# Another written order of the same 1,474 jobs in a fused cosformer-attention and SwiGLU kernel on one core

## The chip, the cores and the metric

One core of a Trainium2 chip runs the whole kernel; the other seven are not used. The metric is the device time of one execution in microseconds. Lower is better. The core's engines are named as in the profile: PE is the matrix engine and PEld its weight load, DVE the vector engine, ACT the scalar engine, POOL the GpSimd engine and SP the sync engine, which here only issues transfers.

## The reference

Linear attention over 8 batches, 8 heads, 576 positions and 64 features per head, and a gated feed-forward block on its result:

```python
def _attn_ref(q, k, v):
    theta = np.pi / 2.0 * np.arange(S) / S              # S = 576
    phi = lambda x: concat([relu(x) * cos(theta), relu(x) * sin(theta)], axis=-1)
    q_p, k_p = phi(q), phi(k)
    kv = einsum('bhsf,bhsd->bhfd', k_p, v)
    den = einsum('bhsf,bhf->bhs', q_p, k_p.sum(axis=2)) + 1e-06
    return einsum('bhsf,bhfd->bhsd', q_p, kv) / den[..., None]

def _moe_ref(x, w_gate, w_val, w_out):                  # x: 4608 x 512
    g = x @ w_gate                                      # 512 x 1536
    return (g * sigmoid(g) * (x @ w_val)) @ w_out       # 1536 x 512
```

The attention output, 4,608 tokens of 512, is the input of the feed-forward block; the result is 4,608 x 512 in float32.

## The kernel before

The 4,608 tokens form nine groups of 512, and a group four tiles of 128. A tile of attention output is a pair of matmul batches into two PSUM banks (`tile_jobs`, lines 768 to 823): PE multiplies the turned query features by the key-value sums, ACT scales the denominators (L803), DVE inverts them (L809) and multiplies (L820), and the tile is turned, by PE for the first tiles (L757) and by a transposing transfer for the others (L749). The key-value sums of a batch are one PE job of 72 small matmuls (`kv_job`, L718) with four casts behind it (L630 on ACT, L634 on DVE). The query features of a batch need its query load (`raw_q`, L125 and L128) and two activations per position slot (L880, L890).

The feed-forward block of the first group is plain: for each of 12 blocks of 128 columns of `w_gate` and `w_val` a PE job of four matmuls each (L917), a SiLU (L925) and a product into `ht` (L937); then 16 jobs of the output product with `w_out` (L1275), cut into four pieces of it by the time at which each piece of `wo_sb` lands. From the second group on the gate and value products (L990) and the output product (L1155) go by a seven-product block scheme, whose sums are made on DVE (L501, L963, L1106, L1010 to L1026) and whose copies are made on ACT (L630).

Up to line 548 the program is written out by hand in one list of words: it loads the first batch, makes the first four attention tiles and blocks 0 to 5 of the first group. All loads of weights and of batches 0 to 2 are issued on POOL ahead of what follows; they share eight completion semaphores, so a load is issued when the eighth before it has landed.

All that comes after is made as jobs, in the order in which the code creates them (number 0 to 1473), and each job has a list of jobs that it must follow. No scheduler runs: a table, `ORDER`, names every job once and so sets what each engine's queue holds and in which order. A word is the job's number, a letter where the job could run on ACT (`a`) or DVE (`v`), and behind the colon the PSUM banks or other places that it takes:

```python
for word in ORDER.split():
    n, e, at = re.match(r"(\d+)([av]?):?([\d,]*)", word).groups()
    j, at = jobs[int(n)], [int(x) for x in (at.split(",") if "," in at else at)]
    j.eng = {"a": "ACT", "v": "DVE", "": next(iter(j.engs))}[e]
    assert j.eng in j.engs and not todo.intersection(j.after + j.behind)
    for r in j.get:
        r.at, at = at[:r.n], at[r.n:]
    todo.remove(j)
    j.fn(j)
```

Each engine works through its own queue in that order. An instruction waits for the semaphores of the instructions that it depends on: its inputs, and those that used its PSUM bank or buffer last. The jobs that the prediction speaks of:

- 4, 8, 12, 16, 20, 24 are the gate products of blocks 6 to 11 of the first group, and 6, 10, 14, 18, 22, 26 the value products (L917). Job 20 is the first that reads the last piece of `wg_sb` (blocks 10 and 11).
- 34 is the key-value sum of batch 1, 35 to 38 its four casts.
- 72, 78, 89, 95 and 104 are the matmuls of attention tiles 4 to 8 (L784), and 67, 84 and 101 turn the queries for them (L1323).
- 39 to 54 are the plain output products (L1275); job 45 is the first that reads the third piece of `wo_sb` (blocks 4 to 7), job 48 the first that reads the last.
- 722 is the key-value sum of batch 6, 723 to 726 its casts, 701 the load of batch 7's query, and 891 an activation that makes features from it (L880).

Of the kernel before, what the change touches and what calls it, by code (L numbers as in the profile page):

```python
# [18 lines left out]
def kernel(  # L19
# [1403 lines left out]
    for tg in range(1, NTG):  # L1423
# [43 lines left out]
        8:7 4:2 12:4 6:1 16:3 10:0 20:5 24:6 5:0 9:5 21:7 13:1 25:3 17:2 29 26:5 22:2 14:7 186 28 7 191 11 31 30 1:0  # L1467
        32 33 67:6 2:4 34:01 68a 70a 38a 35a 36a 37a 223 27 15 219 3 69 71 23 0 39:3 18:5 40:4 78:671 72:120 19 220
        84:5 101:0 79 80 81:0 43 82:6 85a 73 83 87v 187 74 86 75:0 88 188 51:7 42 89:561 45 52 95:120 90 102a 96 91
# [106 lines left out]
```

## Time and profile before

| | before |
|---|---|
| median of 3 runs | 297.64 us |
| the 3 runs | 298.81, 297.64, 297.64 us |
| the profiled execution's own time | 296.95 us |
| its span in the trace | 294.9 us |
| busy PE, DVE, ACT, POOL | 289.7, 253.7, 203.9, 67.9 us |
| granted TensorE clock | 1.00 |
| moved by DMA | 40.91 MB, mean 139 GB/s |

The span runs from the first to the last instruction of the core; the 2.05 us between it and the execution's own time lie around the instructions. PE is counted as busy from a matmul's start to its modelled end, and the matmuls overlap, so a short wait between two of them does not show as idle time in the page; it shows in the timeline as a later start than the rows ahead would give.

### The profile page before, as it was taken

What the parts mean: (1) busy time and instruction counts of PE and PEld (TensorE: products, weight loads), DVE (VectorE), ACT (ScalarE), POOL (GpSimd) and SP (SyncE); (2) the same over time, 40 slices, a digit from 0 to 9 for tenths busy, and PEclk for the clock granted to TensorE, in tenths of its full rate; (3) what the DMA queues carried; (4) which work ended last, traced back from release to release, by engine and by line L of the source; (5) the groups of instructions that cost most, each with busy time, mean ns of one, the idle gap of its engine ahead of it and who ended that gap; (6) DMA issues with size and microseconds to landing.
All of it is one profiled execution on the core that took longest, in us unless ns stands there. A gap on an engine that the chain in (4) does not pass through costs nothing.

```text
span 294.9 us, 8252 instructions
## 1 busy us (share of the span) xinstructions
PE 289.7 (98%) x3328; PEld 241.6 (82%) x3328; DVE 253.7 (86%) x518; ACT 203.9 (69%) x430; POOL 67.9 (23%) x122
## 2 busy tenths in 40 slices
PE   8999999999999999999999999999999999999994
PEld 4597465768888888998898898888988988888883
DVE  8877689999997999999989987998879859966983
ACT  6562556989768987897789589976566275666530
POOL 6763530004008022052215120500050041000200
PEclk9999999999999999999999999999999999999999
DMA  7999999997995997989899994756260343000217
GB/s 252 235 195 198 202 206 208 181 234 113 186 203 134 171 212 111 175 174 172 128 194 198 159 153 81 154 111 83 33 161 19 39 96 86 2 0 2 71 27 190
DMA packets 71974, 40.91 MB, mean 139 GB/s; under 512 B 48768, under 2 KB 68736, under 8 KB 71936
## 3 DMA queue, kind: packets, MB, share of 16 engines
q0 software_dynamic: 24800, 24.39, 48.8%
q1 hardware_dynamic: 46528, 15.47, 28.8%
q10 hardware_dynamic: 608, 0.52, 0.7%
q8 instruction: 26, 0.43, 0.6%
q14 instruction: 12, 0.10, 0.1%
HBM read 37.75 MB, written 9.44 MB: 160 GB/s over the span
## 4 chain that ended last, share of the span: by engine, by line
PE 84%; DMA 14%; issue 0%; DVE 0%; POOL 0%; POOLq 0%
PE banks L990 49%; PE banks L1155 25%; DMA wg_sb<-in_moe_w_gate_dram 7%; DMA wo_sb<-in_moe_w_out_dram 4%; PE banks L1275 3%; PE banks L789 2%; PE banks L718 2%; DMA raw_q<-in_q_dram 2%; DMA wo_sb<-in_v_dram 1%; PE banks L1065 1%; PE banks L757 0%; PE banks L784 0%; DVE r_q L636 0%; POOL hold L469 0%; POOL raw_q L128 0%
## 5 line engine op out<-in xcount | busy, mean ns | idle before, releaser
L1124 POOL DMA_DIRECT2D out_dram<-ob x52 | 27.7, 540 | 125.0 <-ACT ob L632 49.6
L1085 DVE TENSOR_TENSOR ht<-sg,banks 128x512 f16<-128x512 bf16 x69 | 46.4, 681 | 3.3 <-PE banks L990 2.8
L1049 ACT ACTIVATE sg<-banks 128x512 bf16<-128x512 f32 x72 | 42.0, 595 | 6.0 <-PE banks L990 4.7
L630 ACT COPY banks<-banks 128x512 f32<-128x512 f32 (+1 forms) x56 | 31.8, 573 | 16.6 <-PE banks L990 6.1
L990 PEld LDWEIGHTS <-wg_sb 128*128 128x128 f16 x384 | 37.0, 98 | 5.3
L1155 PEld LDWEIGHTS <-ht 128*128 128x128 f16 x384 | 37.2, 98 | 4.6
L990 PEld LDWEIGHTS <-wgs_sb 128*128 128x128 f16 x380 | 36.8, 98 | 4.9 <-issue 0.2
L990 PEld LDWEIGHTS <-wv_sb 128*128 128x128 f16 x368 | 35.6, 98 | 4.3
L1010 DVE TENSOR_TENSOR banks<-m,banks 128x512 f32<-128x512 f32 x47 | 32.4, 691 | 5.5 <-PE banks L990 3.4
L990 PE MATMUL banks<-kvt,wgs_sb 128*128 128x256 f16 x248 | 35.4, 273 | 0.0
L630 ACT COPY m<-banks 128x512 f32<-128x512 f32 x47 | 26.9, 586 | 8.8 <-PE banks L990 7.8
L1155 PEld LDWEIGHTS <-sums 128*128 128x128 f16 x288 | 27.9, 98 | 3.4
L990 PE MATMUL banks<-xT,wg_sb 128*128 128x256 f16 x192 | 28.3, 272 | 0.0
L990 PE MATMUL banks<-xT,wv_sb 128*128 128x256 f16 x184 | 27.6, 273 | 0.0
L1155 PE MATMUL banks<-wo_sb,ht 128*128 128x256 f16 x192 | 24.9, 273 | 0.0
L1155 PE MATMUL banks<-wt_sb,sums 128*128 128x256 f16 x192 | 24.2, 273 | 0.0
L990 PE MATMUL banks<-kvt,wg_sb 128*128 128x256 f16 x168 | 23.9, 273 | 0.0
L632 ACT ACTIVATE ob<-banks 128x512 f32<-128x512 f32 x32 | 19.0, 597 | 7.1 <-PE banks L1155 5.7
L1155 PE MATMUL banks<-wt_sb,ht 128*128 128x256 f16 x192 | 23.2, 273 | 0.0
L820 DVE TENSOR_TENSOR x<-banks,rec 128x512 f16<-128x512 f32 x31 | 21.3, 689 | 1.9
L990 PE MATMUL banks<-kvt,wv_sb 128*128 128x256 f16 x160 | 22.2, 273 | 0.0
L890 ACT ACTIVATE r_q<-raw_q,tanq 128x256 bf16<-128x256 bf16 x45 | 20.5, 500 | 0.8 <-DMA phit<-r_q 0.6
(160 smaller groups left out, 526.1 us busy)
## 6 DMA issues: line engine op xcount, KB each, us to landing
out_dram<-ob POOLq DMA_DIRECT2D x52, 128.0 KB, 3.6
raw_kv<-in_k_dram POOLq DMA_DIRECT2D x7, 576.0 KB, 6.5
raw_q<-in_q_dram POOLq DMA_DIRECT2D x12, 288.0 KB, 10.6
raw_kv<-in_v_dram POOLq DMA_DIRECT2D x6, 576.0 KB, 9.8
out_dram<-ob SPq DMA_DIRECT2D x12, 128.0 KB, 3.0
wg_sb<-in_moe_w_gate_dram POOLq DMA_DIRECT2D x5, 256.0 KB, 9.0
wv_sb<-in_moe_w_val_dram POOLq DMA_DIRECT2D x5, 256.0 KB, 9.4
wo_sb<-in_v_dram SPq DMA_DIRECT2D x2, 576.0 KB, 4.1
```

The lines of the kernel that those rows point to most:

```text
L630: nc.scalar.copy(out=out, in_=in_)
L632: nc.scalar.mul(out=out, in_=in_, mul=mul)
L718: nc.tensor.matmul(out=ps[i * D:(i + 1) * D, e, jj * 2 * D1:(jj + 1) * 2 * D1], lhsT=raws[b, "k"][es, 2 * jj + i, c], rhs=v2s[b == 1][es, ...
L820: tt(out=x_.rearrange("p (i y d) -> p i y d" if pairs else "p (y e d) -> p e y d", d=D, **({"i": 2} if pairs else {"e": 2})), in0=view()[: ...
L890: nc.scalar.activation(out=home()[:, :, c, 1], in_=raws[b, "q"][:, :, c], func=AF.Relu, scale=tanq[:, c:c + 1])
L990: nc.tensor.matmul(out=to[:, i], lhsT=a[:, c, 2 * u + i], rhs=x()[:, :, c], start=first and i == 0 and c == 0, stop=c == KH - 1, skip_grou ...
L1010: tt(out=bank(c), in0=one(m7_all, m).rearrange("p i x -> p (i x)"), in1=bank(b), op=ALU.add)
L1049: nc.scalar.activation(out=gates(rooms[w])[:, :, jh * HT:(jh + 1) * HT], in_=src, func=AF.Silu, scale=DOWN)
L1085: tt(out=ht[:, 4 * u + w:4 * u + w + 3:2, jh * HT:(jh + 1) * HT], in0=gates(rooms[w])[:, :, jh * HT:(jh + 1) * HT], in1=src.rearrange("p ( ...
L1124: {"POOL": nc.gpsimd, "SP": nc.sync, "ACT": nc.scalar}[j.eng].dma_start(out=out_v[idx // NC, idx % NC][:, cols], in_=ob_of(t)[e * SH:(e + ...
L1155: nc.tensor.matmul(out=to, lhsT=a[:, kc, i * P:(i + 1) * P], rhs=b[:, kc], start=first and kc == 0 and i == 0, stop=kc == HC - 1, skip_gro ...
L1275: nc.tensor.matmul(out=bank(tiles[t]), lhsT=ht[:, fc, t * P:(t + 1) * P], rhs=wo_sb[:, fc], start=(fc == 0), stop=(fc == FC - 1))
```

## The change

The table `ORDER` is written anew, nothing else. The same 1,474 jobs stand in it, POOL's and SP's jobs in the same sequence as before, and the jobs of PE, DVE and ACT moved against each other by some places: no PE job moves by more than some 7 us of PE work. Most jobs that take a PSUM bank get another one, and two of the jobs that can run on either engine change it: a cast of batch 1's key-value sums (37) and a ReLU (85) go from ACT to DVE, and another ReLU (87) from DVE to ACT. The first line of the table before and after:

```diff
-        8:7 4:2 12:4 6:1 16:3 10:0 20:5 24:6 5:0 9:5 21:7 13:1 25:3 17:2 29 26:5 22:2 14:7 186 28 7 191 11 31 30 1:0
+        10:0 4:3 8:1 12:2 20:4 24:7 16:5 9:6 5:2 21:0 13:1 25:3 29 17:8 187 28 11 223 219 220 188 31 30 33 1:4 189 32
```

Three places show what that does to an engine's queue. In the rows a name in square brackets is a semaphore that the row waits for: DMASW those of loads issued by POOL, DMAHW those of SP's transfers, the others those of an engine.

PE, where the table's part of the program begins, before. DMASW0 is the landing of the last piece of `wg_sb`, DMASW1 that of the last piece of `wv_sb`:

```order
L917 LDWEIGHTS wg_sb [waits DMASW2_49]
L917 MATMUL banks<-xT,wg_sb 128x512 [waits DVE_49]
...
L917 LDWEIGHTS wg_sb [waits DMASW5_49]
...
L917 LDWEIGHTS wv_sb [waits DMASW3_49]
L917 MATMUL banks<-xT,wv_sb 128x512 [waits DVE_49]
...
L917 LDWEIGHTS wg_sb [waits DMASW0_49]
...
L917 LDWEIGHTS wv_sb [waits DMASW1_49]
```

and with the change:

```order
L917 LDWEIGHTS wv_sb [waits DMASW3_49]
L917 MATMUL banks<-xT,wv_sb 128x512 [waits DVE_49]
...
L917 LDWEIGHTS wg_sb [waits DMASW2_49]
L917 MATMUL banks<-xT,wg_sb 128x512 [waits DVE_49]
...
L917 LDWEIGHTS wg_sb [waits DMASW5_49]
...
L917 LDWEIGHTS wg_sb [waits DMASW0_49]
...
L917 LDWEIGHTS wv_sb [waits DMASW6_49]
```

The row that waits for DMASW0 is job 20. Ahead of it stood 24 matmuls of this list (jobs 8, 4, 12, 6, 16, 10); now 16 stand there (jobs 10, 4, 8, 12). It comes two jobs of four matmuls earlier.

PE, around the first product with the third piece of `wo_sb` (its landing is DMASW0 again), before: the tile of L784 is tile 6, and job 45 follows it.

```order
L784 LDWEIGHTS phit [waits Activation_49]
L784 MATMUL banks<-phit 128x65 [waits DVE_49]
...
L784 LDWEIGHTS phit [waits DVE_49]
...
L1275 LDWEIGHTS ht [waits DMAHW1_49]
L1275 MATMUL banks<-wo_sb,ht 128x512 [waits DMASW0_49]
```

and with the change, from tile 6 on:

```order
L784 LDWEIGHTS phit [waits DVE_49]
L784 MATMUL banks<-phit 128x65 [waits Activation_49]
...
L1323 LDWEIGHTS raw_q
L1323 MATMUL banks<-ident,raw_q 64x128
...
L784 MATMUL banks<-phit 128x65 [waits DVE_49]
...
L1275 LDWEIGHTS ht [waits DMAHW1_49]
L1275 MATMUL banks<-wo_sb,ht 128x512 [waits DMASW0_49]
```

Job 101 (8 small matmuls that turn tile 8's queries) and job 95 (tile 7) now stand between tile 6 and job 45.

ACT, at the first activation on batch 7's query, before. DMASW3 and DMASW2 are the two halves of that load, DMAHW2 the transfer that turns batch 6's features and so frees `r_q`; `kv` are the casts of batch 6:

```order
L630 CAST kv_0_191<-banks 64x4x65 [waits PE_49]
L630 CAST kv_0_191<-banks 64x4x65
L630 COPY banks<-banks 128x512 [waits DVE_49,PE_49]
L1049 ACTIVATE sg<-banks 128x2x256 [waits DVE_49]
L630 CAST kv_0_191<-banks 64x4x65
L880 ACTIVATE r_q<-raw_q,tanq 128x4x64 [waits DMAHW2_49,DMASW3_49,DMASW2_49]
```

and with the change:

```order
L630 CAST kv_0_191<-banks 64x4x65 [waits DVE_49,PE_49]
L630 CAST kv_0_191<-banks 64x4x65
L880 ACTIVATE r_q<-raw_q,tanq 128x4x64 [waits DMAHW2_49,DMASW3_49,DMASW2_49]
L1049 ACTIVATE sg<-banks 128x2x256 [waits PE_49]
L630 COPY banks<-banks 128x512 [waits DVE_49,PE_49]
```

The activation that waits for the load has moved ahead of a copy, a SiLU and a cast, and the key-value job (722) ahead of it stands four products of four matmuls earlier in PE's queue.

More of the change, by code (lines that the diff above doesn't have):

```diff
@@ L1466 @@
     ORDER = """
-        8:7 4:2 12:4 6:1 16:3 10:0 20:5 24:6 5:0 9:5 21:7 13:1 25:3 17:2 29 26:5 22:2 14:7 186 28 7 191 11 31 30 1:0
-        32 33 67:6 2:4 34:01 68a 70a 38a 35a 36a 37a 223 27 15 219 3 69 71 23 0 39:3 18:5 40:4 78:671 72:120 19 220
-        84:5 101:0 79 80 81:0 43 82:6 85a 73 83 87v 187 74 86 75:0 88 188 51:7 42 89:561 45 52 95:120 90 102a 96 91
[64 rows of a table removed]
+        10:0 4:3 8:1 12:2 20:4 24:7 16:5 9:6 5:2 21:0 13:1 25:3 29 17:8 187 28 11 223 219 220 188 31 30 33 1:4 189 32
+        6:2 14:6 22:0 26:1 67:3 34:45 70a 68a 15 7 23 27 69 37v 71 39:6 18:3 2:7 38a 35a 36a 3 0 19 72:450 78:011 79
+        73 80 81:1 84:2 42 40:7 43 82:0 51:3 52 87a 83 85v 74 86 88 75:0 89:011 90 190 186 224 91 92:3 101:2 95:450 45
+        102a 96 41:2 93:0 76:1 48 97 98:1 103 221 94 77 55:0 99:4 104:010 227:5 46 44 57 100 105 122 123 120 228:6 117
[64 rows of a table added]
     """
```

128 rows, old and new, of the table ORDER are left out of this document.

## The prediction

> **What bounds the kernel now.** I read the page's busy times and its chain first, then the windows, then the chain of waits in order of time, and last the timelines of PE, ACT and DVE where the chain leaves PE.
>
> From the page, busy time by engine, and the chain that ended last by engine:
>
> ```profile
> PE 289.7 (98%) x3328; PEld 241.6 (82%) x3328; DVE 253.7 (86%) x518; ACT 203.9 (69%) x430; POOL 67.9 (23%) x122
> PE 84%; DMA 14%; issue 0%; DVE 0%; POOL 0%; POOLq 0%
> ```
>
> PE carries 84% of the chain, transfers 14%, nothing else anything. Three stages of the windows (PE, PEld, DVE, ACT, POOL busy, clock, DMA share, GB/s):
>
> ```profile
> 30.00:40.00 10.00, 10.00 (x128) 5.18 (x126) 7.69 (x16) 5.58 (x11) 6.10 (x9) 1.00 1.31 202
> 100.00:110.00 10.00, 10.00 (x94) 8.96 (x92) 9.93 (x21) 9.05 (x19) 1.49 (x3) 1.00 1.19 193
> 250.00:260.00 10.00, 10.00 (x94) 8.96 (x93) 9.27 (x18) 6.88 (x14) 0.00 (x0) 1.00 0.01 2
> ```
>
> A stage of the block scheme starts 94 matmuls in 10 us at clock 1.00, at 100 us as at 250 us. PE is full, and DVE is nearly full beside it (9.93 of 10). The transfers of the chain, in order of time:
>
> ```profile
> 20.06 11.22 DMA wg_sb<-in_moe_w_gate_dram
> 31.80 12.82 DMA wo_sb<-in_moe_w_out_dram
> 44.66 1.46 PE banks L1275 x6
> ```
>
> The last piece of `wg_sb` lands at 20.06 + 11.22 = 31.28 us, the third piece of `wo_sb` at 31.80 + 12.82 = 44.62 us, and PE's product with it starts 0.04 us later. After that the chain stays on PE to the end. Now PE's timeline across the jobs that the table starts with:
>
> ```profile
> 27.27 2.75 PE L917 MATMUL banks<-xT,wg_sb 128*128 128x512 f16 x12
> 29.86 1.03 PE L917 MATMUL banks<-xT,wv_sb 128*128 128x512 f16 x4
> 32.45 1.89 PE L917 MATMUL banks<-xT,wg_sb 128*128 128x512 f16 x8
> 36.86 0.64 PE L1323 MATMUL banks<-ident,raw_q 128*64 128x128 bf16 x16
> 37.54 1.24 PE L718 MATMUL banks<-phit,raw_kv 64*64 64x130 bf16 x72
> 38.72 0.61 PE L1275 MATMUL banks<-wo_sb,ht 128*128 128x512 f16 x2
> 39.16 1.03 PE L917 MATMUL banks<-xT,wv_sb 128*128 128x512 f16 x4
> 40.02 0.59 PE L1275 MATMUL banks<-wo_sb,ht 128*128 128x512 f16 x2
> 40.55 0.42 PE L784 MATMUL banks<-phit 64*128 64x65 bf16 x16
> 40.90 0.22 PE L784 MATMUL banks<-kvt,phit 64*64 64x65 bf16 x2
> 41.28 0.86 PE L1323 MATMUL banks<-ident,raw_q 128*64 128x128 bf16 x24
> 42.08 0.61 PE L1275 MATMUL banks<-wo_sb,ht 128*128 128x512 f16 x2
> 42.52 0.39 PE L757 MATMUL banks<-ident,x 128*128 128x128 f16 x4
> 42.74 1.03 PE L1275 MATMUL banks<-wo_sb,ht 128*128 128x512 f16 x4
> 43.70 0.20 PE L784 MATMUL banks<-phit 64*128 64x65 bf16 x2
> 44.18 0.39 PE L784 MATMUL banks<-phit 64*128 64x65 bf16 x14 [0.28 <-DVE phit L1339]
> 47.29 1.03 PE L1275 MATMUL banks<-wo_sb,ht 128*128 128x512 f16 x4
> ```
>
> Starts matter here, not busy times. Twelve matmuls from 27.27 to 29.86 give 0.216 us each, or 0.864 us a job. Tile 5 takes 40.90 - 40.55 = 0.35 us; tile 6, begun at 43.70, is followed only at 44.66: 0.61 us lost, part of it to DVE's product at 44.18, the rest to the landing. That is the one wait of size after 27 us. Later ones are small; a typical one of the larger:
>
> ```profile
> 93.23 0.60 PE L990 MATMUL banks<-kvt,wg_sb 128*128 128x256 f16 x4
> 93.80 0.60 PE L990 MATMUL banks<-kvt,wv_sb 128*128 128x256 f16 x4
> ```
>
> Four matmuls at 0.109 us end 0.44 us after their start, and the next start is 0.57 us after: 0.13 us lost. I found some six waits of 0.03 to 0.15 us, 0.5 us in all. So what an order can win is bounded: 0.61 + 0.5, some 1.1 us, unless it shortens what lies ahead of 27.27 us or the jobs themselves, and it touches neither.
>
> The Trainium skill, "Perfetto Trace Analysis", section "Identifying the Most-Contended Engine", calls matmul busy time a bad measure and asks for the busy share of weight loads; by that rule PEld's 82% would leave PE 18% of the span to win. The trace does not bear it out: the starts show PE issuing at one pace almost throughout, at whatever share its weight loads stand.
>
> **The change part by part.** Durations are those of the profiled execution, whose own time is 296.95 us for a span of 294.9; the median of the three runs is 297.64, 0.69 above it, and I carry that difference unchanged.
>
> *First products.* Job 20 comes after 16 matmuls instead of 24: 27.27 + 16 x 0.216 = 30.73 us, where its piece of `wg_sb` lands at 31.28. With the 0.04 us seen at the other landing PE waits **0.59 us**. Before it came at 32.45, 1.17 us after the landing. Job 24 and everything else on PE queues up behind that wait, the value products 6 and 14 that could have filled it among them.
>
> *Third piece of `wo_sb`.* To tile 4 PE has eleven products (11 x 0.864 = 9.50), the first turn with the small product of the tangents (from 36.86 to 37.54, 0.68), the key-value sum (1.18), two output matmuls (0.44) and job 18 (0.86): 12.66 us, so it comes there at 27.27 + 12.66 + 0.59 = 40.52. From there to job 45 stand tile 4 (0.38), three tiles of 0.35, the turns of 24 small matmuls (0.80), one turned tile (0.22) and ten output matmuls (0.24 each as from 42.74 to 43.70, 2.40): 4.85 us, 45.37 us, or 0.75 us after the landing at 44.62. The **0.61 us go**. What would be late next is the last piece, job 48: it stands at 47.29 us before, with no gap ahead of it, and behind job 45 come its 0.86, two output matmuls (0.48) and two turned tiles (0.44): 47.15, within 0.15 us of the old moment. I take nothing.
>
> *First tiles.* A cast of batch 1's sums moves from ACT to DVE, and tile 4 waits for it. DVE's rows there:
>
> ```profile
> 35.50 1.41 DVE L292 TENSOR_TENSOR phit<-raw_kv,tab 128x1152 bf16<-128x1152 bf16 x2
> 37.17 1.27 DVE L937 TENSOR_TENSOR ht<-sg,banks 128x512 f16<-128x512 bf16 x2
> 38.78 0.74 DVE L1339 TENSOR_TENSOR phit<-phit,tanT 128x512 bf16<-128x512 bf16 x2
> ```
>
> From the same 35.50 DVE now does two L292 with a copy of 0.21 and a weight sum of 0.41 among them (1.41 + 0.62 less 0.16 of overlap: 37.37), four L937 (two take 1.27, so 0.60 each: 39.75), one L1339 (0.37) and the cast (ACT does one in 0.38): 40.4 us, against PE's 40.52. It fits by 0.1 us, and only because PE was held 0.59 us; were that wait shorter, this one would take up to 0.4 us of it. Cost zero, bounds 0 and 0.4.
>
> *Batch 7's query.* ACT's first use of it moves ahead. The rows: PE's key-value sum of batch 6, ACT's casts behind it and first use, the two loads, and how long they took:
>
> ```profile
> 167.92 1.25 PE L718 MATMUL banks<-v,raw_kv 64*64 64x130 bf16 x72
> 169.21 0.76 ACT L630 CAST kv<-banks 64x260 bf16<-64x260 f32 x2 [2.38 <-PE banks L718]
> 171.88 0.51 ACT L880 ACTIVATE r_q<-raw_q,tanq 128x256 bf16<-128x256 bf16 x1
> L125 POOL DMA_DIRECT2D raw_q<-in_q_dram x2: 652/664/677, 158.3 to 159.0; - x2
> DMA to landing us min/median/max: 9.5/9.9/10.3
> ```
>
> The query is there by 159.0 + 10.3 = 169.3 us; before, its user came 2.6 us later. Now the key-value sum is four products of 0.44 earlier (166.2), its casts end at 166.2 + 1.29 + 0.76 = 168.2, and ACT then stands 1.1 us waiting for the landing. Queued behind it are a SiLU (0.60) and the copy (0.57) on which an output product on PE waits: ready at 169.3 + 0.41 + 0.50 + 0.57 = 170.8. PE has the 72 small matmuls (1.18) and 40 large ones (4.36) ahead of that product and comes at 166.2 + 5.54 = 171.7. It hides behind 0.9 us of PE work: zero here, and one for one beyond that.
>
> *All the rest*, some 450 PE jobs in a new mixture. A job's inputs come through ACT and DVE in the same counts and at the same durations, so I take the 0.5 us of small waits to stay: zero, with bounds -0.5 (all gone) and +1.0 (three times as many; DVE at 9.93 of 10 has little to catch up with).
>
> **Sum:** 296.95 + 0.59 - 0.61 + 0 = 296.93 in the profiled execution; with 0.69 for the median, 297.62, rounded to **297.7 us** since the uncosted bounds lean upward.
>
> **The rivals.**
>
> *A, slower: the query of batch 7 lands later.* For it: ACT now stands at that wait, with PE's copy behind it. It decides once the load takes more than 10.3 + 0.9 = 11.2 us. All query loads of this execution:
>
> ```profile
> DMA to landing us min/median/max: 6.8/10.2/17.8
> ```
>
> At 14.0 us, midway between 10.3 and the longest, PE loses 2.8 us: 300.5. Against it: POOL's sequence is the same, so the load leaves at the same place among the others. The Trainium skill, "DMA: Bandwidth & Descriptors", section "Issuing engines are not separate DMA queues", has all issuers' transfers run on the same 16 engines and interleave; by that rule the turning transfers of SP, whose sources move, can lengthen this load though POOL's list is unchanged. The spread of 6.8 to 17.8 us agrees.
>
> *B, slower: many small waits.* With DVE near full, eighteen more waits of 0.1 us on PE: 299.5. For it: the order is tight everywhere, and the spare I worked out is 0.1 us at one place, 0.75 and 0.9 at two. Against: before meets its work with six such waits in 264 us, at the same load.
>
> *C, faster:* the ordinary runs, 0.69 us over the profiled one, lose more to the third piece of `wo_sb` than the trace does; that goes, the new wait for `wg_sb` does not come because the first stage ends 0.6 us later there, and the small waits go: 297.64 - 0.69 - 0.61 - 0.4 = 295.9.
>
> *D, no gain but no new wait:* the first stage ends late enough for `wg_sb`, and the rest is as in the trace: 297.64 - 0.6 = 297.0.
>
> *The order does not give late transfers more room:* it does at `wo_sb` (from -0.6 to +0.75), and takes room at `wg_sb` (from +1.2 to -0.6) and the query (from +2.6 to -1.1 on ACT). If all loads are late by x, both orders lose x: this is the forecast itself.
>
> **How the numbers follow.** Forecast 0.58, D 0.10, A 0.12, B 0.12, C 0.08. Within 0.5% (about what a measurement of this kernel can tell from no change; 1.49 us) lie the forecast and D: 0.68. A and B are slower by more: 0.24. C: 0.08. The range leaves out A and C, 0.20, and takes in D, B and the bounds of the terms (297.1 to 298.7): 296.6 to 299.5.
>
> **What would show it right or wrong.** Right: in PE's timeline a gap of about 0.6 us behind the sixteenth L917 matmul, near 30.7 us, ended by `wg_sb`; no gap at the third piece of `wo_sb` near 45.5; ACT idle about 1 us ahead of its first L880, with no gap on PE near 171; 94 matmuls in the windows behind 100 us. Wrong: PE gaps over 0.3 us anywhere else, a chain that leaves PE for ACT or DVE near 170 us, or a start of the table's jobs that is not 27.3 us.

## The result, and the profile after

The changed list takes 301.50 us in the median (298.64 to 306.23), the list before 297.72 (296.88 to 301.07). The ratio of the compared runs is 1.0096, 95% interval 1.0067 to 1.0125. It is nearer to 1 than the ratio of the medians, 1.0127, because it leaves out runs over 1.5% above a kernel's fastest, here five of 20; so the medians are given for every experiment too.

The profiled execution of the changed kernel takes 302.91 us for a span of 301.1, against 296.95 and 294.9 before. Of its page, the busy times, the chain by engine and the granted clock of PE in 40 slices:

```profile
PE 291.5 (97%) x3328; PEld 242.5 (81%) x3328; DVE 255.1 (85%) x519; ACT 203.2 (67%) x429; POOL 67.4 (22%) x122
PE 82%; DMA 12%; DVE 3%; issue 1%; ACT 1%; POOL 0%; DVEq 0%; ACTq 0%
PEclk9999999999799999999999999999999999999999
```

DVE and ACT have come into the chain, and one slice, 75 to 83 us, has a clock of 0.7. The chain of waits in order of time (start, length, what), at the two places where it leaves PE:

```profile
37.87 1.86 DVE ht L937 x3
39.73 0.34 DVE phit L1339
40.07 0.35 DVE phit L634
...
40.50 0.37 ACT phit L630
40.87 0.01 issue
40.88 0.14 ACT phit L630
41.03 0.24 issue
41.27 0.38 ACT phit L630
41.65 0.04 issue
41.70 0.81 PE banks L784 x46
...
69.03 7.29 DMA xT<-x
76.31 0.03 issue
...
76.44 0.70 DVE x L820
77.14 0.04 issue
77.18 3.02 PE banks L990 x17
```

*At 40 us* tile 4 (L784) waits for three casts of ACT, and these wait for the one cast that moved to DVE (L634). All four write parts of one tile, `phit`, and the ACT casts now stand behind the DVE cast in the list. The timeline around it:

```profile
40.00 0.41 DVE L634 CAST phit<-banks 64x260 bf16<-64x260 f32 x1
40.50 1.14 ACT L630 CAST phit<-banks 64x260 bf16<-64x260 f32 x3 [1.36 <-DVE phit L634]
41.70 0.22 PE L784 MATMUL banks<-kvt,phit 64*64 64x65 bf16 x2 [1.00 <-ACT phit L630]
```

PE comes to tile 4 1.07 us later than its queue ahead of it asks for.

*At 69 us* the transposing transfer that turns attention tile 9 (L749, issued by SP) takes 7.29 us. Tile 10's product x (L820) takes the same place of the buffer `x` and waits for that transfer. DVE works in order, so what stands behind L820 waits too, and then PE, at the gate product that is job 405. Job 405 reads tile 9 as well (kernel 13 below shows PE waiting there for the transfer itself), and the transfer lands at 76.32, so the shared place adds 0.86 us at most:

```profile
76.44 0.69 DVE L820 TENSOR_TENSOR x<-banks,rec 128x512 f16<-128x512 f32 x1 [4.06 <-DMA xT<-x]
77.18 0.60 PE L990 MATMUL banks<-xT,wg_sb 128*128 128x256 f16 x4 [3.76 <-DVE x L820]
78.08 1.06 PE L990 MATMUL banks<-kvt,wg_sb 128*128 128x256 f16 x4
```

The last row is the second loss: four matmuls take 1.06 us where 0.60 is usual, and the windows show why (the last three numbers of a row are PE's granted clock, the DMA share and GB/s):

```profile
75.00:77.50 2.50, 0.32 (x3) 0.38 (x4) 1.06 (x2) 0.00 (x0) 0.00 (x0) 1.00 1.21 197
77.50:80.00 2.50, 2.50 (x17) 1.86 (x15) 2.24 (x5) 0.10 (x1) 0.00 (x0) 0.60 1.23 199
80.00:82.50 2.50, 2.50 (x18) 1.99 (x17) 1.73 (x4) 1.32 (x3) 0.00 (x0) 0.71 1.38 174
82.50:85.00 2.50, 2.50 (x25) 2.24 (x24) 2.27 (x5) 1.74 (x4) 0.00 (x0) 1.00 1.19 180
78.10:81.40 3.30, 3.30 (x18) 2.38 (x16) 3.04 (x7) 1.03 (x2) 0.00 (x0) 0.50 1.22 205
```

After 3.76 us without work PE starts 17 and 18 matmuls in a window instead of 25. The last row is the slow stretch alone: from 78.0 to 81.4 us the clock is 0.50, and it fell only 0.8 us after PE had gone on. Four jobs of four matmuls come 0.42 us late each, 1.67 us in all. The Trainium skill, "TensorE: Matmul & The Clock Gate", section "What's actually happening", says that PE's clock is halved after an idle window of about 3.4 us and comes back after about as long a busy one; by that rule a wait of 3.8 us costs some time twice, and the trace agrees, with 3.4 us at half clock.

**The sum.** It is that of one execution. Each job of PE, held against a clock that only adds up the job lengths, gives where it falls back: the first stage ends 0.42 us later (27.69 for 27.27; over all the profiles it ends between 26.8 and 27.8), job 20 waits 0.08, tile 4 1.07, job 405 3.91, the clock 1.67: 7.15 us. The wait at the third piece of `wo_sb` is gone (-0.61), and small waits are 0.34 less. That is 6.20 us, the difference of the spans. Of the 20 runs of the changed list ten have a mean granted clock of 0.994 or less, as this one (0.992), and take 301.46 to 306.23 us; the other ten have 0.998 or more and take 298.64 to 301.54. That suggests that the clock falls in half of the executions; only this one has a profile.

### The profile page after: what moved, and what is told of

The parts are those of the page before. It is cut to its first block, busy times and chain, and to the rows that moved or that the text cites. A ratio compares the mean times of both kernels' runs of the same rounds, so it can differ in the third digit from the quotient of the medians.

```text
span 301.1 us, 8236 instructions
## 1 busy us (share of the span) xinstructions
PE 291.5 (97%) x3328; PEld 242.5 (81%) x3328; DVE 255.1 (85%) x519; ACT 203.2 (67%) x429; POOL 67.4 (22%) x122
## 4 chain that ended last, share of the span: by engine, by line
PE 82%; DMA 12%; DVE 3%; issue 1%; ACT 1%; POOL 0%; DVEq 0%; ACTq 0%
PE banks L990 47%; PE banks L1155 24%; DMA wv_sb<-in_moe_w_val_dram 6%; PE banks L1275 3%; DMA xT<-x 2%; PE banks L718 2%; DMA raw_q<-in_q_dram 2%; PE banks L789 2%; DMA wo_sb<-in_v_dram 1%; PE banks L1065 1%; DVE phit L292 1%; DVE ht L937 1%; PE banks L784 1%; DVE wgs_sb L501 0%; PE banks L757 0%
## 5 line engine op out<-in xcount | busy, mean ns | idle before, releaser
L990 PE MATMUL banks<-kvt,wgs_sb 128*128 128x256 f16 x248 | 36.2, 273 | 0.0
L990 PE MATMUL banks<-xT,wg_sb 128*128 128x256 f16 x192 | 29.0, 275 | 3.8 <-DVE x L820 3.8
L820 DVE TENSOR_TENSOR x<-banks,rec 128x512 f16<-128x512 f32 x31 | 21.3, 689 | 5.9 <-DMA xT<-x 4.1
L990 PE MATMUL banks<-kvt,wg_sb 128*128 128x256 f16 x168 | 25.0, 276 | 0.0
L990 PE MATMUL banks<-kvt,wv_sb 128*128 128x256 f16 x160 | 23.1, 280 | 0.0
L1049 ACT ACTIVATE sg<-m 128x512 bf16<-128x512 f32 x24 | 15.2, 632 | 11.6 <-DVE m L1018 11.5
```

The lines of the kernel that those rows point to most:

```text
L820: tt(out=x_.rearrange("p (i y d) -> p i y d" if pairs else "p (y e d) -> p e y d", d=D, **({"i": 2} if pairs else {"e": 2})), in0=view()[: ...
L990: nc.tensor.matmul(out=to[:, i], lhsT=a[:, c, 2 * u + i], rhs=x()[:, :, c], start=first and i == 0 and c == 0, stop=c == KH - 1, skip_grou ...
L1049: nc.scalar.activation(out=gates(rooms[w])[:, :, jh * HT:(jh + 1) * HT], in_=src, func=AF.Silu, scale=DOWN)
```

## The experiments

Each kernel is one of the two lists with the edits shown; an ORDER word is the job's number, the engine letter and the places. There is no kernel 5. The steps in us that are named for an experiment come from the same reckoning, from its profiled execution. The first theory, X, was the shared place of `x`; C was that the transfer is slow because it meets the loads of batch 3 and of the fourth query, which POOL issues at that moment; M was that without the shared place the wait only moves on to the readers of the turned tiles.

**Kernel 1: place of tile 10.** `150:0` becomes `150:3` in the changed list.

> One place number of the changed table: tile 10's product writes x place 3, free since tile 6, instead of place 0, which tile 9's turning transfer still reads. Theory X (the loss is that wait of DVE, 3.8 us in the profiled execution with the slow PE behind it): the gap near 73 us and the lower clock after it go, and the median comes down from 301.5 to about 298 us, with a spread like that of before. Rival F (the loss lies in the first 45 us, the cast and the weight wait, and the rest only varies): it stays at 300 us or more. Rival M (the wait is moved: tile 10's own transfer is then late for the sums of the third group near 82 us): about 299.5 to 300.5.

Measured: 302.18 us (298.19 to 306.03), ratio 1.0054 (1.0024 to 1.0084). X alone is wrong: tile 10's L820 waits no more, and the times spread as they did. Its profiled execution, 298.19 us, was its fastest and shows no wait over 1 us.

**Kernel 2: place and cast.** Kernel 1, and `37v` becomes `37a`.

> As the run before, and the one cast of batch 1's sums that had gone to DVE is back on ACT. Theory X with the cast as the second term (1.0 us at tile 4): about 297 us, the time of before or 0.3 us either side, PE's gap ahead of tile 4 gone. If the cast costs nothing because the third piece of wo_sb is waited for in its place: the same as the run before, 298.

Measured: 298.52 us (296.53 to 301.95), ratio 1.0017 (0.9992 to 1.0042). That is above the 297 expected, and cannot be told from before.

**Kernel 3: cast alone.** `37v` becomes `37a` in the changed list.

> The changed table with the cast alone back on ACT, x place as in the changed table. Theory X: the gap near 73 us stays, so about 300.5 us, 1 us better than the changed table. Rival F: most of the loss goes, 298.5 us or less.

Measured: 298.39 us (296.89 to 304.59), ratio 1.0001 (0.9973 to 1.0030). One letter takes away 3.1 of the 3.8 us, though its own place accounts for 0.8: tile 4's step falls from 1.07 to 0.28. By the numbers this is F's forecast (298.5 or less) and not X's; what the cast has to do with the rest comes with kernels 11 to 15. The timeline shows the step, and the wait for `wg_sb` that the prediction had forecast, here 0.94 us with the first stage ending early, at 26.92:

```profile
31.47 0.82 PE L917 MATMUL banks<-xT,wg_sb 128*128 128x512 f16 x3 [0.94 <-DMA wg_sb<-in_moe_w_gate_dram]
41.15 0.22 PE L784 MATMUL banks<-kvt,phit 64*64 64x65 bf16 x2 [0.20 <-ACT phit L630]
```

**Kernel 6: loads later.** In the changed list `138 146` becomes `146 138` and the instruction that holds those loads back on POOL (L837) reads tile 9's turned slot instead of tile 8's, so the loads cannot start before tile 9 is turned.

> The changed table with the shared x place, but the loads of batch 3 and of the fourth query are held on POOL until tile 9's turning transfer has landed, instead of tile 8's. Every engine's instructions are in the same order. Theory C (the wait is long because that transfer runs beside these loads: 7.3 us against 2.4 in before): the transfer takes about 2.5 us, DVE's wait near 73 us nearly goes, and the median falls to 298 to 299 us even with the shared place. Rival P (the place alone decides, whatever else moves): no change, 301 us.

Measured: 298.71 us with the narrowest spread of the kernels that ran twelve times, 298.32 to 299.57; ratio 1.0031 (1.0014 to 1.0047). Its transfer of tile 9 takes 2.4 us, and no wait stands at job 405, shared place or not. C holds; the local wait at tile 4 is still there (0.96).

**Kernels 7 to 9 and 4: combinations.** Kernel 7 is the changed list with all three edits (place, cast, loads later); kernel 9 is kernel 7 with `20:4 24:7 16:5 9:6` as `16:5 9:6 20:4 24:7`; kernel 8 is the list before with the loads later; kernel 4 is the list before with tile 10 in tile 9's place (`150:2` becomes `150:3`).

> The changed list with three edits: tile 10's x in a place of its own turn (3), the cast of batch 1's sums for job 37 back on ACT, and the loads of batch 3 and the fourth query held until tile 9's x is turned. From 298.7 of the third edit alone, the cast gives back 0.7 (the step at tile 4 falls from 0.96 to 0.28), and the place nothing more: 297.9 to 298.2, with a spread under 1.5 us. Rival (the list loses by many small waits everywhere): 298.5 or more. Rival (the later loads make their readers late once tile 10 no longer waits): over 299.

> The seventh kernel (place, cast, loads later) with jobs 16 and 9 ahead of job 20, so that 24 matmuls stand before the first reader of the last piece of wg_sb as in before. If the wait at that piece is what is left of the list's loss, 0.8 to 1.0 us less than the seventh: 296.9 to 297.3, at or under before's 297.65. Rival: the wait is only moved (PE runs into tile 4's or the batch-1 chain's inputs, whose time is set by DVE and ACT and not by PE): the same as the seventh within 0.3 us.

> The kernel before, with the loads of batch 3 and the fourth query held until tile 9's x is turned instead of tile 8's, and issued behind that transfer. If the collision of turning transfers with these loads also causes the longer runs of before (up to 299 to 301), they go: spread under 1.5 us around 297 to 297.8. If before's longer runs have another cause, spread and median stay (297.6, up to 299). If the later loads are late for their readers, over 298.5.

> The kernel before, with one number changed: tile 10's x takes the place of tile 9's (as in the changed list) instead of tile 8's old turn. Theory X+C (the shared place is a wait only when tile 9's turning transfer is caught among the loads of batch 3): in executions where that transfer lands in the 2.4 us of the profile before, nothing is lost; where it takes 7 us or more, DVE stands up to 4 us and PE with it. So a median 0.3 to 3 us above before and a longest run 4 us or more above the shortest. Rival (the shared place is only a wait in the changed list, because there the loads start closer to the transfer): within 0.3 us of before, spread as before's.

Measured: kernel 7 298.29 us (297.39 to 302.66), ratio 1.0011 (0.9980 to 1.0042); kernel 9 298.19 (297.15 to 299.37), 1.0015 (0.9995 to 1.0035); kernel 8 297.91 (296.85 to 299.15), 0.9985 (0.9953 to 1.0017); kernel 4 298.16 (296.67 to 300.26), 1.0005 (0.9973 to 1.0037). Nothing here can be told from before. Kernel 7's median is 0.1 us above what was expected, but its spread is 5.3 us and not under 1.5; its two runs over 301 us have a granted clock of 1.00 and the loads held, so they most likely have another cause, which stays open. And the later loads have a price in the profiles, here kernel 7's:

```profile
92.91 0.60 PE L990 MATMUL banks<-kvt,wgs_sb 128*128 128x256 f16 x4 [0.94 <-ACT banks L630]
```

ACT's copy stands there behind an activation that waited 1.42 us for a transposing transfer of features. Kernels 6, 9 and 10 show the same wait of PE (0.93 to 1.05 us); kernel 2, which is kernel 7 without the later loads, does not. In kernel 9, 20 matmuls stand ahead of job 20 and not the 24 of the expectation, since job 9 is a SiLU on ACT. They took the wait for `wg_sb` away, but job 6 behind it then waited 0.48 us for ACT, and nothing was won. In before's list the loads issued later win nothing that can be told (the spread is 2.3 us; before's own longest run in that comparison, 301.66 us, has no profile), and the shared place costs nothing that can be told.

**Kernel 10: place and loads later, cast on DVE.**

> The changed list with tile 10's x in place 3 and the loads of batch 3 and the fourth query held until tile 9's x is turned (the cast stays on DVE). If what is left in the runs of 302 to 306 of the first kernel, in which the place was already free, is still the meeting of the turning transfers with these loads: 298.3 to 299 with a spread under 1.5 us, as with the later loads alone (298.7). If it has another cause: median 300 or more, up to 304.

Measured: 299.29 us (298.37 to 300.73), ratio 1.0053 (1.0033 to 1.0072): the runs of 302 to 306 of kernel 1 are gone. The median is a little above the 298.3 to 299 expected; in the profile PE waits 1.60 us for `wg_sb` and loses 0.96 us at tile 4.

**Kernel 11: the cast alone in the list before.** `37a` becomes `37v`.

> The kernel before with one letter changed: the cast of batch 1's sums for job 37 on DVE instead of ACT, at the same place of the list. In before's list this job stands behind its three ACT casts, so they do not wait for it: if the loss at tile 4 comes from ACT's casts standing behind the one of DVE in the list, within 0.4 us of before. Rival (DVE itself is late there and anything moved to it is late): 0.7 to 1.1 us above before, 298.3 to 298.8. Rival (a late tile 4 makes the later transfers meet the loads, whatever the list): a median 2 us or more above before.

Measured: 305.74 us (304.21 to 306.83), ratio 1.0261 (1.0231 to 1.0292). This one letter costs 8 us. The first expectation was wrong, and at the cast's own place too: there DVE's cast stands behind ACT's casts (second view), a product of DVE comes late, and PE waits for it (first view). The last expectation, 2 us or more, held: the larger part is a step of 4.30 us at job 405, where PE stands for tile 9's transfer. The views are the timeline, the groups by line from 36 to 43 us, and then SP's transfers of `xT` and POOL's loads between 67.5 and 70.5 us (the times after the durations are the first and the last start):

```profile
40.66 1.02 PE L917 MATMUL banks<-xT,wv_sb 128*128 128x512 f16 x4 [1.39 <-DVE ht L937]
```

```profile
L634 DVE CAST phit<-banks 64x260 bf16<-64x260 f32 x1 | 0.4, 423 | 2.1 <-ACT phit L630 2.1
```

```profile
L749 SPq DMA_TRANSPOSE xT<-x x1: 1205/1205/1205, 69.9 to 69.9; - x1
  PE banks L990: 4.1, 1
DMA to landing us min/median/max: 9.8/9.8/9.8
```

```profile
L120 POOL DMA_DIRECT2D raw_kv<-in_k_dram x1: 748/748/748, 69.1 to 69.1; - x1
```

The transfer starts 0.8 us behind the first load and takes 9.8 us. In the profile before, the same two views, for 67.5 to 69.5 us:

```profile
L749 SPq DMA_TRANSPOSE xT<-x x1: 1189/1189/1189, 68.0 to 68.0; - x1
DMA to landing us min/median/max: 2.4/2.4/2.4
```

```profile
L120 POOL DMA_DIRECT2D raw_kv<-in_k_dram x1: 832/832/832, 68.5 to 68.5; - x1
```

There it starts 0.5 us ahead of the load and takes 2.4 us. So a third theory, O: what decides is which of the two is issued first.

**Kernels 12 and 13: kernel 1 again, for two more profiles.**

> The first kernel again (tile 10's x in place 3 and nothing else), to see one of its runs of over 301 in a profile. If the wait moved to the readers of the turned tiles: a transfer of a turned tile 9, 10 or 11 of 7 us or more, PE idle for 2 us or more between 72 and 95 us behind kvt (L963) or xT, and a granted clock under 0.9 behind it. If the loss lies elsewhere (the first stage, the last batches): PE without a gap over 1 us in that stretch.

> The same kernel once more, for a second profile: as for the run before it.

Measured: 298.56 and 305.14 us. The same program shows both cases. In the long execution PE waits at job 405 for the transfer itself, place or no place, and all that it does from there to 83.8 us runs at a clock of 0.50:

```profile
78.49 1.01 PE L990 MATMUL banks<-xT,wg_sb 128*128 128x256 f16 x4 [4.41 <-DMA xT<-x]
```

```profile
78.50:83.80 5.30, 5.30 (x26) 3.77 (x27) 2.55 (x5) 1.03 (x2) 0.00 (x0) 0.50 1.33 169
```

The profiles up to here in which the loads were not held longer, by the distance of the two issues (tile 9's transfer less the first load of batch 3); a step of 0 is one under 0.06 us:

| Kernel | transfer less load, us | transfer took, us | step at job 405, us |
|---|---|---|---|
| 2 (place, cast) | -0.78 | 2.4 | 0 |
| 4 (before, shared place) | -0.70 | 2.4 | 0 |
| before | -0.55 | 2.4 | 0 |
| 1 (place) | -0.23 | 4.4 | 0.29 |
| 3 (cast) | -0.22 | 4.4 | 1.00 |
| 12 (place) | -0.17 | 5.2 | 1.12 |
| after | +0.32 | 7.3 | 3.91 |
| 13 (place) | +0.52 | 8.7 | 4.56 |
| 11 (before, cast on DVE) | +0.88 | 9.8 | 4.30 |

In these nine the duration grows with the distance, and the margin of before is half a microsecond. The Trainium skill, "DMA: Bandwidth & Descriptors", section "Issuing engines are not separate DMA queues", has transfers of all issuers interleave on the same 16 engines; the table agrees, and adds that a lead of 0.55 us was enough to be spared and one of 0.17 to 0.23 us was not.

**Kernel 14: kernel 11 with the loads later.**

> The kernel before with both edits: job 37's cast on DVE (alone 305.7) and the loads of batch 3 and the fourth query held until tile 9's x is turned (alone 297.9). Theory O (the cast alone costs some 2.5 us by itself; the rest of its 8 us comes because tile 9's transfer, one to two us later, is issued behind the loads instead of ahead of them): 299.5 to 301, with PE going on at job 405 within 1.5 us of its place and no granted clock under 0.9 at 80 us. Rival (the cast makes DVE late all along and the transfer is only where it shows): 304 or more.

Measured: 300.19 us (299.68 to 300.84), ratio 1.0084 (1.0063 to 1.0105). The cast stays as late as it was (the steps at 40 us are the same), the transfer takes 2.4 us again, the windows at 80 us have a clock of 1.00, and 5.5 of the 8 us are gone:

```profile
L749 SPq DMA_TRANSPOSE xT<-x x1: 1189/1189/1189, 70.0 to 70.0; - x1
DMA to landing us min/median/max: 2.4/2.4/2.4
```

```profile
80.00:82.50 2.50, 2.37 (x22) 1.95 (x21) 2.43 (x5) 2.30 (x6) 0.00 (x0) 1.00 1.24 174
```

**Kernel 15: the flip alone, in the list before.** `144 145:3 138 146 139 247:0 157 154` becomes `247:0 157 144 145:3 138 146 139 154`.

> The kernel before with four DVE jobs of batch 3's time in another order: the bank and feature products 247 and 157 stand ahead of tile 9's two (144, 145), so that tile 9's x is ready some 1.9 us later (69.9 instead of 67.99 us) and its turning transfer is issued behind the first load of batch 3 (68.5) instead of 0.5 us ahead of it; nothing is late before that. Theory O (that order decides): the transfer takes 7 to 10 us instead of 2.4, PE stands 2 to 4.5 us at job 405 with a granted clock under 0.8 behind it, a median of 300.5 to 304. Rival (the transfer is only where a lateness from the first stage shows): within 0.5 us of before.

Measured: 304.92 us (303.79 to 305.63), ratio 1.0232 (1.0203 to 1.0261). The transfer starts at 69.67, 1.08 us behind the load, and takes 9.6 us. It is not a pure flip: the moved DVE jobs also make PE wait 1.36 us at 69.70, and the median lies above the 304 expected by less than that. Most of the rest is the wait of 4.34 us and the clock behind it:

```profile
69.70 0.61 PE L990 MATMUL banks<-xT,wg_sb 128*128 128x256 f16 x4 [1.36 <-DVE x L820]
79.30 1.04 PE L990 MATMUL banks<-xT,wg_sb 128*128 128x256 f16 x4 [4.34 <-DMA xT<-x]
80.13 1.06 PE L990 MATMUL banks<-kvt,wv_sb 128*128 128x256 f16 x4
```

**Kernel 16: the changed list with its two early losses mended.** `37v` becomes `37a`, and jobs 16 and 9 stand ahead of 20 as in kernel 9.

> The changed list with its two losses in the first 42 us mended and nothing else: job 37's cast back on ACT, and jobs 16 and 9 ahead of job 20. Places and loads as in the changed list. If those two are all that the list loses, and the rest of its order is as good as before's: 297.2 to 298.2, within 0.3% of before, with single runs over 300 where the transfer still falls behind the loads. Rival (the rest of the order loses by itself): 298.7 or more.

Measured: 298.31 us (297.34 to 302.73), ratio 1.0015 (0.9991 to 1.0040). Its transfer started 0.29 us ahead of the load and took 4.3 us; the step at job 405 was 0.87. The median is 0.1 us above the range expected. The rest of the changed order is as good as before's within what can be told, and no version beat the list before by more than can be told.

**Why a lateness near 40 us turns the order round.** The loads start at a pace of their own: POOL waits for tile 8's transfer, and that stands on SP behind one transposing transfer of features (L852) and six stores. SP's timeline, of before and then of kernel 11 (start, length):

```profile
53.67 7.39 SPq L852 DMA_TRANSPOSE phit<-r_q  x1
61.16 4.20 SPq L1124 DMA_DIRECT2D out_dram<-ob  x6
65.41 3.77 SPq L749 DMA_TRANSPOSE xT<-x  x2
```

```profile
55.66 5.71 SPq L852 DMA_TRANSPOSE phit<-r_q  x1
61.47 3.72 SPq L1124 DMA_DIRECT2D out_dram<-ob  x6
65.24 5.91 SPq L749 DMA_TRANSPOSE xT<-x  x2
```

The features come 2.0 us later in kernel 11, but their issue is shorter and ends at 61.4 us against 61.1; tile 8's transfer starts at 65.2 against 65.4, and the load at 69.1 against 68.5. Tile 9's product hangs on PE and DVE, and comes 1.9 us later. Why L852 lets go of SP near 61 us in all of them was not tested.

## Why the prediction was wrong

Forecast were 297.7 us, with 296.6 to 299.5; measured 301.50. The time came from two steps of the working.

*First products* held as a rule: PE waits until the piece of `wg_sb` is there. The size depends on two moments that vary between executions, the end of the first stage and the landing: 0.59 us were forecast for 27.27 and 31.28, 0.08 came in the profiled execution (27.69 and 31.18), and between nothing (kernel 1) and 1.76 us (kernel 10) in the others with 16 matmuls ahead of job 20.

*Third piece of `wo_sb`* held: the 0.61 us are gone, and no wait took their place. PE came to job 45 at 46.54 us, behind the old landing as well as the new one, 43.42.

*First tiles* failed, cost 0 with bounds 0 and 0.4. DVE's cast was worked out to end at 40.4 us (the terms as given add up to 40.5) and ended at 40.41. What the step left out is that the three casts that stayed on ACT write the same tile and stand behind it: 1.07 us at tile 4. That was in the list: the three words follow `37v`.

*Batch 7's query* held at zero. In the profiled execution even the wait that was to hide did not come, because the losses ahead had made ACT's casts later (174.5 us) than the landing (173.9). In kernel 16, whose list is the same there, it came, 0.87 us, and hid as worked out: PE shows no wait near 171 us. ACT's timeline of the changed list, and then kernel 16's:

```profile
173.71 0.76 ACT L630 CAST kv<-banks 64x260 bf16<-64x260 f32 x2 [0.31 <-PE banks L718]
174.37 0.51 ACT L880 ACTIVATE r_q<-raw_q,tanq 128x256 bf16<-128x256 bf16 x1
```

```profile
170.86 0.51 ACT L880 ACTIVATE r_q<-raw_q,tanq 128x256 bf16<-128x256 bf16 x1 [0.87 <-DMA raw_q<-in_q_dram]
```

*All the rest* is the step that failed most: zero, bounded by -0.5 and +1.0, since "a job's inputs come through ACT and DVE in the same counts and at the same durations". Tile 9's input to job 405 comes through a transfer, whose duration was not fixed: 2.4 us ahead of the loads, 7 to 10 behind them. The wait and the clock behind it cost 3.91 + 1.67 = 5.6 us in the profiled execution. The margin, half a microsecond between two issues at 68.0 and 68.5 us, could have been read in the trace before; the bound of +1.0 counted only waits on PE, ACT and DVE.

None of the rivals had this. *A* named the mechanism, transfers that lengthen each other, but for the loads as the victims and for batch 7; that its 300.5 came nearest to 301.50 is luck. *B*'s 299.5 was wrong on the cause too: the loss is mostly one wait and the clock behind it, not eighteen small ones.

## What to carry to other kernels

In a hand-written order, look for pairs of transfers whose issue is set by two different engines, and read how many tenths of a microsecond lie between them: a short transfer whose reader waits must be issued ahead of bulk loads, and a dependency that holds the loads is safer than a lead of half a microsecond, at a price (here a wait of PE of some 1 us near 93 us in the changed list). Where jobs on two engines write parts of one tile, moving one of them makes the others wait in list order. A long wait of PE can cost more than its length: here those of 3.8 us and more did, and those of up to 1.6 us did not; nothing between was measured.

## What had not been expected of the hardware

Less than a microsecond in the moment of issue changed the same transposing transfer from 2.4 to 7.3 us and more, and a lateness of 2.5 us became 8 us of execution. The granted clock fell to 0.50 where PE stood 3.8 to 4.4 us: for 3.4 us in the profiles of the changed list and of kernels 11 and 15, which cost 1.7 us each time, and for 6.8 us in kernel 13, where it fell before PE went on and cost some 2.6 us (an estimate: half of the 5.3 us that PE worked at it). Waits of 1.0 to 1.6 us left it at 1.00. And issuing one transposing transfer held SP for 5.7 and 7.4 us at L852 in the two rows above and for 1.3 to 12.6 us over all the profiles, where those of L749 took 1.2 to 2.5.
